# The softmax weights P of a top-k attention transposed by DMA through a DRAM scratch, in 26 of 32 head pairs, instead of by TensorE

## The chip, the cores and the metric

The kernel runs on one core of one Trainium2 chip. The metric is the device time of one execution in microseconds (us), the median over several runs. Five engines work side by side, each through its own instructions in order: TensorE (PE, with its weight loads shown apart as PEld), VectorE (DVE), ScalarE (ACT), GpSimd (POOL) and SyncE (SP), which here only issues DMAs. An engine waits only where its next instruction needs something that another engine or a DMA has not finished.

## The reference

Attention over 8 batches of 8 heads, 576 tokens, head size 64, in which each query keeps its 32 largest scores; then a Fourier mixing of the result and a two-layer MLP. All in 32-bit floats.

```python
scores = q @ k.T / sqrt(64)                      # per head: 576 x 576
kth = the 32nd largest score of each row
scores = where(scores >= kth, scores, -1e9)
attn = softmax(scores)                           # P, up to its denominator
x = (attn @ v) laid out as (batch, 576, 8 * 64)

mixed = real(fft(fft(x, axis=tokens), axis=channels))
u = x + mixed
un = (u - mean(u)) / sqrt(var(u) + 1e-6)
out = u + relu(un @ w_ch1) @ w_ch2               # 512 -> 2048 -> 512
```

## The kernel before

**Tiles.** The 64 heads are taken as 32 pairs, four pairs a batch. A pair is nine tiles of 128 query rows by 576 keys: blocks t = 0, 1, 2, 3 of 128 queries for head e = 0 and head e = 1, and one tile (t = 4, e None) that holds the last 64 queries of both heads. The order in a pair is t = 0, 0, 1, 1, 4, 2, 2, 3, 3. A batch has 36 tiles, the kernel 288.

**What happens to a tile.** PE computes the scores into PSUM (L369, and L339 for the last 64 keys), ACT copies them to SBUF as `S` (L372, L343, L361). DVE finds the 32 largest of each row: four MAX8 (L393) with three MATCH_REPLACE8 (L395) between them, writing to the work tile `wk`. `bounds` (L402, POOL) makes two numbers a row of the result. `mask` writes a large value to `wk` where the score is under the bound (Relu on ACT, L409) and subtracts that from the score (POOL, L412). `expo` (ACT, L418) takes the exponential in place in `wk`, with the row's sum. This is P, not yet normalised, with queries on the partitions.

The product with v needs P with keys on the partitions. `transposes` has PE transpose 128x128 blocks against an identity into PSUM (L439, four a tile; L450 and L454 for the last 64 keys) and ACT copy them to `PT` (L442, L451, L455, L457). `PT` has one buffer for each of two chunks of a pair: chunk 0 holds t = 0, 1, 4 (320 queries), chunk 1 holds t = 2, 3 (256 queries); each has nine blocks of 128 keys, four a head and one that both heads' last 64 keys share. `attend` (L476) multiplies PT by v in 20 matmuls into the PSUM tile `o`; ACT copies o to `xT` (L490); PE transposes it back (L516) and DVE normalises it into `x`.

**The Fourier part and the MLP** of a batch run while later batches are in attention: the foldings on POOL, the small transforms on PE (L667, L728), the MLP in units that the planner counts at about 1.8 to 2.7 us (`hidden`, L878, whose result ACT takes out of PSUM at L882; `back`, L905 and L944; and, once a batch, a product made of seven part products, L1075, for which halves and combinations of w2 are loaded again from DRAM by `bring`, L821).

**What sets the order.** The program is written out by hand for every engine, one step i a tile. In step i, PE computes the scores of tile i+3; ACT and POOL mask tile i-1 and take its exponential; PE transposes tile i-2; at the end of the step, if tile i-3 was the last of a chunk (position 4 or 8 in its pair), `attend` follows and ACT copies o to xT; DVE runs the last rounds of tile i and the first of tile i+1. Between these a planner places MLP units: `level` chooses a length for the step such that the queued units fit until the next batch's arrive, and `fixed_cost` is what it thinks PE needs for the attention work of a step (0.55 us of it for the transposes). In the first batch the transposes come a step earlier.

**Queues and buffers.** After the start, all loads and stores go through SP's queue, in program order: eight loads each of q, k and v for a pair (L236, L252, into the single buffer `nat`, or one of two of v), the MLP's w2 parts and the results. `S` has six buffers, `wk` three of a pair of tiles (one more for t = 4). PSUM has two banks for scores, two for transposes, one for `o`, three for the MLP.

Of the kernel before, what the change touches and what calls it, by code (L numbers as in the profile page):

```python
# [9 lines left out]
F32 = mybir.dt.float32  # L10
I32 = mybir.dt.int32
U32 = mybir.dt.uint32
AF = mybir.ActivationFunctionType
ALU = mybir.AluOpType

# [3 lines left out]
P = 128  # L19
TH = 32  # L20
# [52 lines left out]
def kernel(  # L73
# [9 lines left out]
    nc = tc.nc  # L83
    B, H, S, D = q.shape
# [5 lines left out]
    NF = NC - 1  # L90
    TAIL = 2 * TH
# [3 lines left out]
    NPB = H // 2  # L95
    NPAIR = B * NPB
# [5 lines left out]
    CW = (2 * P + TAIL, 2 * P)  # L102
    CHUNK_OF = {0: (0, 0), 1: (0, P), 4: (0, 2 * P), 2: (1, 0), 3: (1, P)}
# [10 lines left out]
    attp = ctx.enter_context(tc.tile_pool(name="attp", bufs=2))  # L114
    batp = ctx.enter_context(tc.tile_pool(name="batp", bufs=1))
    small = ctx.enter_context(tc.tile_pool(name="small", bufs=4))
    dramp = ctx.enter_context(
        tc.tile_pool(name="dram", bufs=1, space=bass.MemoryType.DRAM)
    )
# [53 lines left out]
    def weight_steps(chunks, space, wc, slots):  # L173

        def words(n):
            o = 2 * wc * (n % slots)
            raw = space[:, o:o + 2 * wc]
            return raw, raw[:, 0:2 * wc:2], raw[:, 1:2 * wc:2]
# [9 lines left out]
        def scale_high(n):  # L188
            if moe_w_ch1.dtype == F32:
                return  # L190
            nc.scalar.activation(
                out=chunks[n][0], in_=words(n)[2], func=AF.Copy, scale=2.0 ** -112
            )
# [9 lines left out]
        def rest(n):  # L203
            if moe_w_ch1.dtype == F32:
                return
            _, low, high = words(n)
            nc.scalar.activation(
                out=low.bitcast(I32), in_=low.bitcast(U32), func=AF.Copy, scale=2.0 ** -29
            )
            nc.scalar.activation(out=high, in_=high.bitcast(I32), func=AF.Sign)  # L210

# [13 lines left out]
    nat, qT_of, kT_of, v_of, PT, Ssb, Wk, Wp, M8, Nt = ({} for _ in range(10))  # L225
# [76 lines left out]
    PER_PAIR = len(IN_PAIR)  # L302
# [3 lines left out]
    items = [(pair, t, e) for pair in range(NPAIR) for t, e in IN_PAIR]  # L306
    N = len(items)
# [90 lines left out]
    def bounds(i):  # L398

        if i < N:  # L400
# [2 lines left out]
                out=Nt[i], in0=M8.pop(i)[:, 0:TOPK:TOPK - 1], in1=cc, op=ALU.mult  # L403
            )

    def mask(i, then=None):

        w = Wk[i]
        nc.scalar.activation(out=w, in_=Ssb[i], func=AF.Relu, scale=-FAR, bias=Nt[i][:, 1:2])  # L409
        if then is not None:  # L410
            then()
        nc.gpsimd.tensor_tensor(out=w, in0=Ssb.pop(i), in1=w, op=ALU.subtract)  # L412

    def expo(i):
        pair, t, e = items[i]
        w = Wk[i]
        c = DEN_COL[(t, e)]
        nc.scalar.activation(  # L418
            out=w, in_=w, func=AF.Exp, bias=Nt.pop(i)[:, 0:1],
            accum_out=den_t[pair % 3][:, c:c + 1],  # L420
        )

    def transposes(i):


        pair, t, e = items[i]
        p_sb = Wk.pop(i)
        ch, col = CHUNK_OF[t]
        if (pair, ch) not in PT:
            PT[pair, ch] = attp.tile(  # L430
                [P, 2 * NF + 1, CW[ch]], F32, name=f"PT_{pair}_{ch}", tag=f"PT{ch}", bufs=1
            )
        pt = PT[pair, ch]

        def full():
            k0 = TAIL if e == 1 else 0
            tp = ps_t.tile([P, 4, P], F32, name=f"tpP_{i}", tag="tp")
            for c in range(NF):
                nc.tensor.transpose(tp[:, c, :], p_sb[:, k0 + P * c:k0 + P * (c + 1)], ident)  # L439
            dsts = [(e, 0, P)] if e is not None else [(0, 0, TAIL), (1, TAIL, TAIL)]  # L440
            for he, o, w in dsts:
                nc.scalar.copy(  # L442
                    out=pt[:, NF * he:NF * (he + 1), col:col + w], in_=tp[:, :, o:o + w]
                )

        def tails():
            tp = ps_t.tile([P, 4, P], F32, name=f"tpP_{i}_t", tag="tp")
            if e == 1:
                both = Wp.pop(i - 1).rearrange("p e s -> p (e s)")[:, NF * P:S + TAIL]
                nc.tensor.transpose(tp[:, 0, :], both, ident)  # L450
                nc.scalar.copy(out=pt[:, 2 * NF, col:col + P], in_=tp[:, 0, :])  # L451
                return
            Wp.pop(i)
            nc.tensor.transpose(tp[:, 0, :], p_sb[:, S - P:S], ident)  # L454
            nc.scalar.copy(out=pt[TAIL:P, 2 * NF, col:col + TAIL], in_=tp[TAIL:P, 0, TAIL:P])  # L455
            for r in (0, TH):
                nc.scalar.copy(  # L457
                    out=pt[r:r + TH, 2 * NF, col:col + TAIL],
                    in_=tp[TAIL + r:TAIL + r + TH, 0, 0:TAIL],
                )  # L460

        full()
        if e != 0:
            tails()
        return 0.48 if e == 0 else 0.6

    def attend(pair, ch, c0=0, c1=None):

        c1 = CW[ch] if c1 is None else c1
        pt, vv = PT[pair, ch], v_of[pair]  # L470
        if c0 == 0:
            o_of[pair, ch] = ps_o.tile([P, CW[0]], F32, name=f"o_{pair}_{ch}", tag="o")
        o = o_of[pair, ch]
        for c in range(NC):
            for e in range(2):
                nc.tensor.matmul(  # L476
                    o[D * e:D * (e + 1), c0:c1],
                    lhsT=vv[:, c, e, :],
                    rhs=pt[:, 2 * NF if c == NF else NF * e + c, c0:c1],
                    start=(c == 0),  # L480
                    stop=(c == NC - 1),
                )
        return (c1 - c0) / 115.0

    def attended(pair, ch, late):
# [15 lines left out]

        nc.scalar.activation(out=rd[:, 0:n], in_=den[:, c0:c0 + n], func=AF.Copy, bias=1e-9)
        late.append(lambda: nc.vector.reciprocal(out=rd[:, 0:n], in_=rd[:, 0:n]))
# [780 lines left out]
    for o, place in ((B12, w2_12), (B21, w2_21)):  # L1284
        at(PER_BATCH + 14, "load2", lambda o=o, place=place: nc.sync.dma_start(
            out=scr[:, o], in_=place
# [3 lines left out]
    for b in range(B):  # L1290
# [47 lines left out]
        for n, t in enumerate((0, 1, 4, 2, 3)):  # L1338
            quick = first or last
            s = fc + (0 if first else n // 3 if last else n // 2)  # L1340
# [13 lines left out]

    def fixed_cost(i):

        t = 0.55 if 0 <= i - 2 < N else 0.0
        if i + 3 < N:
            t += {0: 1.04, 1: 0.3, None: 0.9}[items[i + 3][2]]
        if 0 <= i - 3 < N:  # L1360
            ch = {4: 0, 8: 1}.get((i - 3) % PER_PAIR)
            t += 0.0 if ch is None else (CW[ch] / 115.0 + 0.14 * len(CHUNKS[ch]))
        if i < N and i % PER_PAIR in (0, 5):
            t += 0.7
        return t + costs.get(i, 0.0)

    def level(i):

        steps = range(i, next((a for a in arrivals if a > i), i + PER_BATCH))
        rest, lev = sum(u[0] for u in queue + waiting), 0.0  # L1370
        while lev < 6.4 and sum(max(0.0, lev - fixed_cost(s)) for s in steps) < rest:
            lev += 0.02
        return lev

    def run(i, where):
        for fn in plan.pop((i, where), []):
            fn()
# [15 lines left out]
    i, carry = 0, 0.0  # L1393
    while i < N + 4 or plan or queue or sums:
# [3 lines left out]

        short = 0 <= i - 1 < PER_BATCH
        done = i - 1 if short else i - 2 if PER_BATCH <= i - 2 < N else None  # L1400

        fixed, j = [], i + 3
        e = items[j][2] if j < N else None
# [13 lines left out]
        if pending and pending[0][0] <= i and (  # L1419
            i < 2 * PER_BATCH + 4 or (i - 3) % PER_PAIR not in (4, 8)  # L1420
        ):
            _, pp, pc = pending[0]
# [12 lines left out]
        if short:  # L1435
            fixed += tok
            pair, r = divmod(i - 1, PER_PAIR)
            piece = {1: (0, 0, P), 4: (0, P, CW[0]), 6: (1, 0, P), 8: (1, P, CW[1])}.get(r)
            if piece is not None:
                fixed.append(lambda: attend(pair, *piece))  # L1440
            if i == PER_BATCH:
                fixed.append(lambda: attended(NPB - 1, 1, late_next) or 0.0)
                fixed.append(lambda: to_tokens(NPB - 1, 1, False))
        if i in arrivals:
            carry = min(carry, 0.0) if i > arrivals[0] else -5.0
            run(i, "units")
            step_us = level(i)
        room = step_us - carry - fixed_cost(i)
        cost, got = carry, 0.0
        run(i, "convert")  # L1450
        if short:
            expo(i - 1)
        for n, fn in enumerate(fixed):
            cost += fn()
            if n == n_mask:
                if PER_BATCH <= i - 1 < N:
                    mask(i - 1)
                run(i, "act")
                for fn in out_next:
                    fn()  # L1460
                out_next.clear()
            if n == min(n_tr, len(fixed) - 1) and PER_BATCH <= i - 1 < N:
                expo(i - 1)

            got += some(max(room * (n + 1) / len(fixed) - got, 1.1 if fn in preps else 0.0))
        if short:
            if piece is not None and r in (4, 8) and i < PER_BATCH:

                out_next.append(lambda pc=(pair, r // 8): attended(*pc, late_next))
                pending.append((i + 1, pair, r // 8))  # L1470

        soon_tile = 2 * PER_BATCH - 1
        for tile in (i - 3, i - 2):
            if not PER_BATCH <= tile < N or (tile == i - 2) != (tile == soon_tile):
                continue
            pair, r = divmod(tile, PER_PAIR)
# [27 lines left out]
        if i < PER_BATCH:  # L1504
            mask(i, lambda: run(i, "join"))
# [45 lines left out]
```

## Time and profile before

| | us |
|---|---|
| median of three runs | 1904.74 (1903.89 to 1906.25) |
| the profiled execution | 1907.16 |
| its span on the core | 1905.4 |
| period of a middle batch (36 tiles) | 214.4 |
| MAX8 and MATCH_REPLACE8 of one tile (three MAX8 of 0.749, one of 0.743, three MATCH_REPLACE8 of 0.742) | 5.2 |
| one exponential, with its accumulator read | 0.780 + 0.194 |
| one subtraction on POOL (L412) | 1.416 |
| one copy of four transposed blocks from PSUM to PT (L442, 512 columns) | 0.587 |

The mean granted TensorE clock of the profiled execution is 0.969 of full speed.

A page of the profile gives the busy time of each engine and its share of the span; the span in 40 slices, where a digit is the busy share in tenths; groups of instructions of one line with their count, their busy time in us, the mean duration of one in ns, and the idle time of the engine just before them with what ended it; and the DMA issues by line with KB each and the median us from issue to landing. Busy time of a group counts overlapping instructions once, so it is less than count times mean where instructions are pipelined, as on PE. A second kind of view gives the busy time of each engine in a stretch of the span, with the granted clock and the share of time that the 16 DMA engines were busy. A timeline gives start and duration of single instructions.

### The profile page before, as it was taken

Reading aid. Unit: us, or ns where it says so; the run is one execution under the profiler, and the core shown is the slowest. Engines: PE = TensorE matmul, PEld = TensorE weight load, DVE = VectorE, ACT = ScalarE, POOL = GpSimd, SP = SyncE. Lnnn points to the kernel's source line nnn. Section 1 sums busy time; section 2 is a strip of 40 time slices with the busy share of each in tenths; the row PEclk is TensorE's granted clock in tenths of the full one; section 3 lists DMA queues with packets and bytes.
Section 4 is the critical chain, followed back from the end, with each engine's and each line's share of the span. In section 5 each row is a group of like instructions: output and inputs, shape, how many; then the busy total and the mean of one; then the engine's idle time right before and its main releaser. Section 6 shows DMA issues by size and latency. Waiting matters only on the chain.

```text
span 1905.4 us, 28704 instructions
## 1 busy us (share of the span) xinstructions
PE 1790.4 (94%) x9200; PEld 1182.4 (62%) x9200; DVE 1585.3 (83%) x3301; ACT 1208.5 (63%) x3078; POOL 908.4 (48%) x1278
## 2 busy tenths in 40 slices
PE   5567799999899999999999999999999999999999
PEld 3344465474567756667567656667567656667678
DVE  7999999999899999989899888989899888872110
ACT  6878657776766767657676667666676667652100
POOL 4768643556535374345534464245534464241022
PEclk7787899999999999999999999999999999999999
DMA  5333001311104111131113101141113102030132
GB/s 165 104 94 108 20 13 50 99 56 25 41 14 130 34 25 47 42 107 28 25 47 98 53 20 52 35 114 27 25 47 97 53 19 57 25 103 6 50 101 80
DMA packets 184342, 111.25 MB, mean 58 GB/s; under 512 B 125952, under 2 KB 174208, under 8 KB 184192
## 3 DMA queue, kind: packets, MB, share of 16 engines
q1 hardware_dynamic: 183408, 109.20, 20.3%
q8 instruction: 74, 1.21, 0.3%
q14 instruction: 76, 0.62, 0.1%
q10 hardware_dynamic: 784, 0.21, 0.0%
HBM read 93.63 MB, written 15.73 MB: 57 GB/s over the span
## 4 chain that ended last, share of the span: by engine, by line
PE 80%; ACT 8%; DVE 6%; POOL 3%; issue 1%; DMA 1%; SPq 1%; POOLq 0%; DVEq 0%; ACTq 0%
PE hp L878 26%; PE cp L905 10%; PE o L476 8%; PE tpP L439 6%; PE sp L369 5%; PE cw L1075 5%; PE cv L1075 4%; PE yp L667 3%; PE cp L944 3%; DVE m L393 2%; DVE wk L395 2%; PE sp_t L339 2%; PE mp L728 2%; POOL wk L412 1%; ACT wk L409 1%
## 5 line engine op out<-in xcount | busy, mean ns | idle before, releaser
L412 POOL TENSOR_TENSOR wk<-S,wk 128x576 f32<-128x576 f32 x288 | 407.7, 1416 | 731.8 <-ACT wk L409 701.2
L393 DVE MAX8 m<-wk 128x8 f32<-128x576 f32 x864 | 626.3, 749 | 6.1
L878 PE MATMUL hp<-unT,w 128*128 128x256 f32 (+1 forms) x2048 | 539.9, 410 | 2.6 <-ACT unT L796 2.6
L878 PEld LDWEIGHTS hp<-unT,w 128*128 128x128 f32 x2048 | 374.3, 191 | 124.7 <-issue 25.8
L395 DVE MATCH_REPLACE8 wk<-m,wk 128x576 f32<-128x576 f32 x576 | 427.6, 742 | 0.0
L418 ACT ACTIVATE wk<-wk,nt 128x576 f32<-128x576 f32 x288 | 224.7, 780 | 75.6 <-POOL wk L412 74.5
L409 ACT ACTIVATE wk<-S,nt 128x576 f32<-128x576 f32 x288 | 226.8, 787 | 36.2 <-POOL nt L402 35.2
L439 PE MATMUL tpP<-ident,wk 128*128 128x128 f32 x1152 | 183.9, 284 | 67.3 <-ACT wk L418 40.7
L905 PE MATMUL cp<-w,hT 128*128 128x512 f32 x512 | 240.6, 598 | 0.0
L442 ACT COPY PT<-tpP 128x512 f32<-128x512 f32 (+1 forms) x320 | 171.2, 547 | 106.8 <-PE tpP L439 104.3
L393 DVE MAX8 m<-S 128x8 f32<-128x576 f32 x288 | 214.0, 743 | 21.6 <-ACT S L343 21.6
L439 PEld LDWEIGHTS tpP<-ident,wk 128*128 128x128 f32 x1152 | 141.2, 145 | 141.2 <-ACT wk L418 64.2
L882 ACT ACTIVATE hT<-hp 128x320 f32<-128x320 f32 (+1 forms) x256 | 104.7, 409 | 194.5 <-PE hp L878 192.1
L395 DVE MATCH_REPLACE8 wk<-m,S 128x576 f32<-128x576 f32 x288 | 213.7, 742 | 0.0
L476 PE MATMUL o<-PT,v 128*64 128x256 f32 (+3 forms) x1440 | 195.2, 414 | 1.9 <-ACT PT L442 1.8
L372 ACT COPY S<-sp 128x512 f32<-128x512 f32 (+1 forms) x264 | 141.7, 588 | 48.9 <-PE sp L369 48.6
L369 PE MATMUL sp<-kT,qT 64*128 64x512 f32 (+1 forms) x528 | 160.2, 666 | 4.8 <-ACT means L1263 3.3
L476 PEld LDWEIGHTS o<-PT,v 128*64 128x64 f32 x1440 | 111.4, 152 | 73.8 <-issue 16.7
L905 PEld LDWEIGHTS cp<-w,hT 128*128 128x128 f32 x512 | 88.8, 190 | 86.3 <-issue 86.2
L1020 POOL TENSOR_TENSOR hT<-hT 128x512 f32<-128x512 f32 x64 | 81.4, 1275 | 100.3 <-ACT hT L882 88.6
L1075 PE MATMUL cw<-w,hT 128*128 128x256 f32 x448 | 106.7, 383 | 1.4 <-POOL nt L402 1.2
L1075 PEld LDWEIGHTS cw<-w,hT 128*128 128x128 f32 x448 | 81.4, 190 | 18.9 <-issue 5.2
(157 smaller groups left out, 2179.3 us busy)
## 6 DMA issues: line engine op xcount, KB each, us to landing
w<-w_parts SPq DMA_DIRECT2D x82, 512.0 KB, 4.4
space<-in_moe_w_ch_dram SPq DMA_DIRECT2D x32, 512.0 KB, 3.5
nat<-in_q_dram SPq DMA_DIRECT2D x128, 64.0 KB, 2.1
v<-in_v_dram SPq DMA_DIRECT2D x128, 64.0 KB, 2.2
out_dram<-x SPq DMA_DIRECT2D x32, 256.0 KB, 2.1
nat<-in_k_dram SPq DMA_DIRECT2D x124, 64.0 KB, 2.2
w_parts<-w_t SPq DMA_DIRECT2D x8, 512.0 KB, 2.9
w_s<-w_parts SPq DMA_DIRECT2D x8, 512.0 KB, 4.8
```

What stands on the lines that cost most here:

```text
L369: nc.tensor.matmul(sp[r], lhsT=qT[hd, q_cols], rhs=kT[hd, :], start=True, stop=True)
L393: ops.append(lambda src=src, m8=m8: nc.vector.max(out=m8, in_=src))
L395: ops.append(lambda src=src, m8=m8: nc.vector.match_replace(w, m8, src, NEG))
L409: nc.scalar.activation(out=w, in_=Ssb[i], func=AF.Relu, scale=-FAR, bias=Nt[i][:, 1:2])
L412: nc.gpsimd.tensor_tensor(out=w, in0=Ssb.pop(i), in1=w, op=ALU.subtract)
L418: nc.scalar.activation(out=w, in_=w, func=AF.Exp, bias=Nt.pop(i)[:, 0:1], accum_out=den_t[pair % 3][:, c:c + 1],)
L439: nc.tensor.transpose(tp[:, c, :], p_sb[:, k0 + P * c:k0 + P * (c + 1)], ident)
L442: nc.scalar.copy(out=pt[:, NF * he:NF * (he + 1), col:col + w], in_=tp[:, :, o:o + w])
L476: nc.tensor.matmul(o[D * e:D * (e + 1), c0:c1], lhsT=vv[:, c, e, :], rhs=pt[:, 2 * NF if c == NF else NF * e + c, c0:c1], start=(c == 0), ...
L878: nc.tensor.matmul(hp[:, 0:w], lhsT=w1[:, dt, P * it:P * (it + 1)], rhs=unT[:, dt, 0:w], start=(dt == 0), stop=(dt == NDT - 1),)
L905: nc.tensor.matmul(cp, lhsT=hT[:, it, P * n:P * (n + 1)], rhs=w2[:, it, :], start=(it == 0), stop=(it == NIT - 1),)
L1075: nc.tensor.matmul(dst, lhsT=h()[a][:, kc, :], rhs=rhs_of(kc), start=start and kc == 0, stop=kc == NK - 1, skip_group_check=True,)
```

## The change

In pairs 4 to 30 except pair 7 (26 of 32), P is transposed by DMA. `expo` writes P not to `wk` but over the scores in `S`. `plane` copies it back to `wk` as two planes: first all low, then all high 16-bit halves of the row's 576 words, two strided copies on ACT, the first at the end of the step of the exponential (for tile i-1), the second at the start of the next (for tile i-2). It then writes the planes to a DRAM scratch in which a row is one query: 2 planes of 1152 values, the 576 of head 0 and the 576 of head 1 side by side (for t = 4 three writes bring the two heads together). After the second head, `turn` issues one DMA transpose of the (query, plane) rows, 256 rows of 1152 16-bit values (128 for t = 4), straight to PT, where low and high halves come to lie beside each other and form the 32-bit words again. All of these go through SP's queue. In those pairs `transposes` is not called: neither its PE transposes nor its ACT copies are there. The order of the instructions around them changes with it: the exponential now follows the last of a step's fixed PE pieces, which is often the only one. The shared block of PT moves from last to the middle, for all pairs. `fixed_cost` leaves out the 0.55 us in the pairs that changed. `attend` stays at its place.

```diff
--- before.py
+++ after.py
@@ -10,6 +10,7 @@
 F32 = mybir.dt.float32
 I32 = mybir.dt.int32
 U32 = mybir.dt.uint32
+U16 = mybir.dt.uint16
 AF = mybir.ActivationFunctionType
 ALU = mybir.AluOpType

@@ -403,21 +404,74 @@
                 out=Nt[i], in0=M8.pop(i)[:, 0:TOPK:TOPK - 1], in1=cc, op=ALU.mult
             )

+    def by_dma(i):
+
+        pair = i // PER_PAIR
+        return NPB <= pair < NPAIR - 1 and pair != 2 * NPB - 1
+
     def mask(i, then=None):

         w = Wk[i]
         nc.scalar.activation(out=w, in_=Ssb[i], func=AF.Relu, scale=-FAR, bias=Nt[i][:, 1:2])
         if then is not None:
             then()
-        nc.gpsimd.tensor_tensor(out=w, in0=Ssb.pop(i), in1=w, op=ALU.subtract)
+        nc.gpsimd.tensor_tensor(out=w, in0=Ssb[i], in1=w, op=ALU.subtract)
+        if not by_dma(i):
+            Ssb.pop(i)

     def expo(i):
         pair, t, e = items[i]
         w = Wk[i]
         c = DEN_COL[(t, e)]
         nc.scalar.activation(
-            out=w, in_=w, func=AF.Exp, bias=Nt.pop(i)[:, 0:1],
+            out=Ssb[i] if by_dma(i) else w, in_=w, func=AF.Exp, bias=Nt.pop(i)[:, 0:1],
             accum_out=den_t[pair % 3][:, c:c + 1],
+        )
+
+    planes_of = {}
+
+    def plane(i, half):
+
+        if not (0 <= i < N and by_dma(i)):
+            return
+        words = Wk[i].bitcast(U16).rearrange("p (h s) -> p h s", h=2)
+        src = Ssb[i].bitcast(U16).rearrange("p (s h) -> p h s", h=2)
+        nc.scalar.copy(out=words[:, half, :], in_=src[:, half, :])
+        if half == 0:
+            return
+        Ssb.pop(i)
+        Wk.pop(i)
+        pair, t, e = items[i]
+        nq = TAIL if e is None else P
+        if e != 1:
+            planes_of[pair, t] = dramp.tile(
+                [nq, 2, 2 * S], U16, name=f"planes_{pair}_{t}", tag="planes", bufs=3
+            )
+        to = planes_of[pair, t]
+        if e is not None:
+            nc.sync.dma_start(out=to[:, :, S * e:S * (e + 1)], in_=words)
+        else:
+            nc.sync.dma_start(out=to[:, :, 0:S], in_=words[0:nq])
+            nc.sync.dma_start(out=to[:, :, S:S + TAIL], in_=words[nq:P, :, NF * P:S])
+            nc.sync.dma_start(out=to[:, :, S + TAIL:2 * S], in_=words[nq:P, :, 0:NF * P])
+        if e != 1:
+            Wp.pop(i)
+
+    def turn(i):
+
+        if not (0 <= i < N and by_dma(i)) or items[i][2] == 0:
+            return
+        pair, t, e = items[i]
+        src = planes_of.pop((pair, t))
+        ch, col = CHUNK_OF[t]
+        if (pair, ch) not in PT:
+            PT[pair, ch] = attp.tile(
+                [P, 2 * NF + 1, CW[ch]], F32, name=f"PT_{pair}_{ch}", tag=f"PT{ch}", bufs=1
+            )
+        pt, nq = PT[pair, ch], src.shape[0]
+        nc.sync.dma_start_transpose(
+            out=pt[:, :, col:col + nq].bitcast(U16),
+            in_=src.rearrange("q h s -> (q h) s"),
         )

     def transposes(i):
@@ -440,7 +494,7 @@
             dsts = [(e, 0, P)] if e is not None else [(0, 0, TAIL), (1, TAIL, TAIL)]
             for he, o, w in dsts:
                 nc.scalar.copy(
-                    out=pt[:, NF * he:NF * (he + 1), col:col + w], in_=tp[:, :, o:o + w]
+                    out=pt[:, (NF + 1) * he:(NF + 1) * he + NF, col:col + w], in_=tp[:, :, o:o + w]
                 )

         def tails():
@@ -448,14 +502,14 @@
             if e == 1:
                 both = Wp.pop(i - 1).rearrange("p e s -> p (e s)")[:, NF * P:S + TAIL]
                 nc.tensor.transpose(tp[:, 0, :], both, ident)
-                nc.scalar.copy(out=pt[:, 2 * NF, col:col + P], in_=tp[:, 0, :])
+                nc.scalar.copy(out=pt[:, NF, col:col + P], in_=tp[:, 0, :])
                 return
             Wp.pop(i)
             nc.tensor.transpose(tp[:, 0, :], p_sb[:, S - P:S], ident)
-            nc.scalar.copy(out=pt[TAIL:P, 2 * NF, col:col + TAIL], in_=tp[TAIL:P, 0, TAIL:P])
+            nc.scalar.copy(out=pt[TAIL:P, NF, col:col + TAIL], in_=tp[TAIL:P, 0, TAIL:P])
             for r in (0, TH):
                 nc.scalar.copy(
-                    out=pt[r:r + TH, 2 * NF, col:col + TAIL],
+                    out=pt[r:r + TH, NF, col:col + TAIL],
                     in_=tp[TAIL + r:TAIL + r + TH, 0, 0:TAIL],
                 )

@@ -476,7 +530,7 @@
                 nc.tensor.matmul(
                     o[D * e:D * (e + 1), c0:c1],
                     lhsT=vv[:, c, e, :],
-                    rhs=pt[:, 2 * NF if c == NF else NF * e + c, c0:c1],
+                    rhs=pt[:, NF if c == NF else (NF + 1) * e + c, c0:c1],
                     start=(c == 0),
                     stop=(c == NC - 1),
                 )
@@ -1354,7 +1408,7 @@

     def fixed_cost(i):

-        t = 0.55 if 0 <= i - 2 < N else 0.0
+        t = 0.55 if 0 <= i - 2 < N and not by_dma(i - 2) else 0.0
         if i + 3 < N:
             t += {0: 1.04, 1: 0.3, None: 0.9}[items[i + 3][2]]
         if 0 <= i - 3 < N:
@@ -1398,6 +1452,8 @@

         short = 0 <= i - 1 < PER_BATCH
         done = i - 1 if short else i - 2 if PER_BATCH <= i - 2 < N else None
+        if done is not None and by_dma(done):
+            done = None

@@ -1447,6 +1503,8 @@
             step_us = level(i)
         room = step_us - carry - fixed_cost(i)
         cost, got = carry, 0.0
+        plane(i - 2, 1)
+        turn(i - 2)
         run(i, "convert")
         if short:
             expo(i - 1)
@@ -1469,6 +1527,7 @@
                 out_next.append(lambda pc=(pair, r // 8): attended(*pc, late_next))
                 pending.append((i + 1, pair, r // 8))

+        plane(i - 1, 0)
         soon_tile = 2 * PER_BATCH - 1
         for tile in (i - 3, i - 2):
             if not PER_BATCH <= tile < N or (tile == i - 2) != (tile == soon_tile):
```

## The prediction

> **What bounds the kernel now.** I read the page's busy shares and its slices first, then the busy time of single batches, then the waits of one middle batch.
>
> ```profile
> PE 1790.4 (94%) x9200; PEld 1182.4 (62%) x9200; DVE 1585.3 (83%) x3301; ACT 1208.5 (63%) x3078; POOL 908.4 (48%) x1278
> ...
> PE   5567799999899999999999999999999999999999
> ...
> DVE  7999999999899999989899888989899888872110
> ```
>
> DVE is full for 36 of 40 slices and stops where attention stops (near 1714 us); the last 190 us are TensorE alone and the change does not touch them. The shares of the whole span therefore hide what matters. By stretches (length, then PE, PEld, DVE, ACT, POOL busy, clock, DMA share, GB/s; second batch, third batch, one middle batch, last batch):
>
> ```profile
> 240.00:470.00 230.00, 219.68 (x1071) 132.89 (x1070) 216.29 (x447) 155.67 (x421) 112.02 (x162) 0.99 0.17 49
> 470.00:686.00 216.00, 207.09 (x1119) 139.68 (x1121) 201.94 (x419) 148.33 (x386) 107.70 (x164) 0.98 0.20 52
> 936.05:1150.47 214.42, 213.15 (x1131) 141.29 (x1132) 192.71 (x401) 145.40 (x372) 104.61 (x156) 1.00 0.19 51
> 1542.00:1714.00 172.00, 170.50 (x889) 111.04 (x888) 143.81 (x300) 108.37 (x276) 77.66 (x107) 1.00 0.19 53
> ```
>
> A middle batch takes 214.4 us for 36 tiles (5.96 us a tile). PE is busy 99% of it and sets the time; DVE follows at 90%, ACT at 68%. So work taken off PE shortens the batch, but only until the next engine is full: never below DVE's 192.7.
>
> **The change, part by part** (per middle batch of 4 pairs; 26 pairs change in all).
>
> *Removed from PE.* Groups of the same middle batch and of the page:
>
> ```profile
> L439 PE MATMUL tpP<-ident,wk 128*128 128x128 f32 x144 | 21.7, 273 | 0.0
> L450 PE MATMUL tpP_t<-ident,wk 128*128 128x128 f32 x16 | 4.4, 273 | 0.0
> L454 PE MATMUL tpP_t<-ident,wk 128*128 128x128 f32 x4 | 1.1, 273 | 0.0
> ```
>
> 21.7 + 4.4 + 1.1 = 27.2 us of PE's path; PE falls to 213.2 - 27.2 = 186 us and stops being the longest.
>
> *Removed from and added to ACT.* The instructions that write PT are 68 ACT copies, 26.5 us of busy time in that batch. Added are two copies of 128x576 16-bit values for each of 36 tiles. The trace has no such copy; the nearest is a copy from SBUF to SBUF that reads every second word and converts integers:
>
> ```profile
> L207 ACT ACTIVATE space<-space 128x512 int32<-128x512 uint32 x32 | 21.4, 669 | 0.0
> ...
> L418 ACT ACTIVATE wk<-wk,nt 128x576 f32<-128x576 f32 x288 | 224.7, 780 | 75.6 <-POOL wk L412 74.5
> ```
>
> 669 ns at 512 columns, plus 64 columns at 0.83 ns (L442 takes 587 ns at 512 columns and 386 at 256, 0.8 ns a column), is 0.72 us. Bounds: 0.59 us (a 512-wide copy out of PSUM) and 0.97 (the exponential with its accumulator read, 780 + 194 ns). I take 0.72, less 0.03 because neighbours overlap (two copies of 588 ns end in 1.06 us): 72 x 0.69 = 49.7. ACT's busy time goes 145.4 - 26.5 + 49.7 = 168.6 us.
>
> *A wait that comes with it.* The exponential of a tile needs POOL's subtraction, which needs ACT's own Relu:
>
> ```profile
> 999.57 0.80 ACT L409 ACTIVATE wk<-S,nt 128x576 f32<-128x576 f32 x1
> ...
> 1000.45 1.41 POOL L412 TENSOR_TENSOR wk<-S,wk 128x576 f32<-128x576 f32 x1 [3.25 <-ACT wk L409]
> ...
> 1001.90 0.78 ACT L418 ACTIVATE wk<-wk,nt 128x576 f32<-128x576 f32 x1 [1.05 <-POOL wk L412]
> ```
>
> From Relu's end (1000.37) to the exponential's start is 1.53 us, in which ACT idles unless other copies stand between. PT copies often stood there; now the exponential is issued straight after the Relu in 14 of a batch's 36 tiles. Taking 1.53 less the ACT work between the two, tile by tile in the instruction order, gives 34 us a batch after and 12 before; the trace shows 7.2 of those 12. I take 28 (bounds 20, the measured ratio, and 34). Behind the waiting exponential stand the Relus of the hidden layer and the score copies, so PE waits for PSUM banks next. ACT's own floor is 168.6 + 28 + 4.8 (the wait for o before xT that it has today) = 201 us: above DVE's 192.7 and PE's 186. ACT becomes the longest.
>
> *Added DMAs.* Per batch 32 writes of 288 KB and 12 smaller ones to DRAM, and 20 transposes, 16 of 576 KB and 4 of half that, all on SP's queue. How long a plain DMA takes is in the issues; how much a packet costs is in two stretches, 1013.5 to 1018.5 us (only 256-byte rows in flight) and 1023 to 1044 us (1 KB rows):
>
> ```profile
> out_dram<-x SPq DMA_DIRECT2D x32, 256.0 KB, 2.1
> nat<-in_k_dram SPq DMA_DIRECT2D x124, 8.0 KB, 1.7
> ```
> ```profile
> q1 hardware_dynamic: 1278, 0.30, 26.5%
> ```
> ```profile
> q1 hardware_dynamic: 2783, 2.77, 46.6%
> ```
>
> 16 engines x 5 us x 0.265 / 1278 = 16.6 ns for a 256-byte packet; 16 x 21 x 0.466 / 2783 = 56 ns for 1 KB. No row shows a DMA transpose. If it reads its 576 KB as 2304 packets of 256 bytes, that is 2304 x 16.6 / 16 = 2.4 us, plus the 1.7 us that an 8 KB load needs to land: 4.1 us. Bounds: 3.3 (576 KB at the best slice, 359 GB/s, plus 1.7) and 9.8 (each packet at the 56 ns of a 1 KB one, 8.1 + 1.7). I take 4.1, the row of the same packet size, and keep both ends. Bandwidth is no limit at that price: 36 tiles x 256 packets x 63 ns / 16 = 36 us and 18 x 2.4 = 43 us beside today's 0.19 x 214 = 41, 120 us of some 207.
>
> One rule speaks against the change: the Trainium skill, "VectorE: DVE Perf Modes", section "The three transpose paths", puts a 128x128 two-byte block at 390 ns on TensorE and 1309 ns by DMA, and recommends TensorE where PSUM will do. TensorE's row here is 21.7 / 144 = 0.15 us for a whole 32-bit block; a transpose of the change holds 18 two-byte blocks, so by the page, with nothing overlapping, it would take 23.6 us and the kernel would end near 2,840 us. I do not take it: 1.3 us for one small DMA is less than the 1.7 us of the smallest loads here, so most of it must be fixed cost, paid once a DMA.
>
> *Whether the transposes arrive in time.* A tile's second plane copy opens step i, the attend that needs it closes step i+1: two steps, 11.5 us at 207 us a batch. In them lie the copy 0.7, the write's landing 2.1, the transpose 4.1 and the attend's 20 matmuls 2.9 (ACT waits for them at xT): 9.8. SP must also issue eight q, k or v loads ahead of some of these, 0.48 us each:
>
> ```profile
> 1013.75 1.92 SPq L236 DMA_DIRECT2D nat<-in_k_dram  x4
> ```
>
> That is 3.8 us, of which I let 1.0 fall into the chain: 10.8, leaving 0.7 us. The write also frees the tile's half of wk, where a transpose on PE did; with three pairs of wk in rotation its next user comes six steps later, which covers it. S is freed a step later, and its next writer is ACT itself, later in ACT's own order: nothing. The loads themselves, needed four or more steps later, are covered by that distance; the reloads of w2 halves that queue behind a transpose have two or more product parts between load and use. If the cover is gone, every microsecond late is paid by ACT and PE at both chunks of a pair: 52 us of span per us, at most.
>
> **The sum.** Three engines now stand at 186, 193 and 201 us; today's idle DVE time (21.7 us) shows how loosely they run, and I add a quarter of it, 5.5: 207 us a middle batch, 7.4 less. The planner's 0.55 us less a step spreads the same MLP units and moves no work between batches. Four such batches give 30. The third batch has 9 us more DVE work (201.9): 210, 6 less. The second (three pairs changed, DVE already 94%) 4 less. The last (three pairs) 7.4 x 27/36, 5 less. Together 45: the profiled span of 1905.4 becomes 1860. That execution took 1907.2, the runs' median is 1904.7; 45 less is **1860 us**. Its own range: 198 us a middle batch (DVE, with a quarter of its idle time) gives -92 in all, 1813; 212 gives about -14, 1890.
>
> **Rivals.**
> *Late transposes.* The wait for DMA takes the place of the transposes on PE. For it: no row prices a transpose, the slack is 0.7 us, and SP's queue holds loads, writes and transposes in one order, each transpose waiting for its write. Against it: 256-byte packets are cheap here. It decides from 0.9 us late on (45 / 52), a transpose of 5.7 us. At 7 us it is 2.2 late, 114 us: 1975. At the bound of 9.8 it is 5 late, 260 us: 2120.
> *ACT is fuller still.* At 0.97 us a plane copy ACT's floor is 219, the batch 222, some 50 us more than before over six and a half batches: 1955. For it: 72 copies replace 68, of twice the length; against: ACT's conversion copy above shows 669 ns.
> *Nothing is left of it.* Relief on PE is eaten by ACT's waits and by small delays of attends: 214 us a batch, 1905. For it: the floor of 201 is only 6% away; against: PE's 27 us is really gone.
>
> **How the numbers follow.** The forecast has 0.46, all faster. Late transposes 0.32, slower. ACT fuller 0.12, of which 0.10 slower and 0.02 faster. Nothing left 0.10: 0.05 within 0.2%, about what a measurement tells from no change, 0.03 slower, 0.02 faster. So faster 0.50, same 0.05, slower 0.45. The likeliest case is 1860 (1813 to 1890); for 8 in 10 the range must reach into the late transposes, to 2050 (a transpose of some 8.4 us), leaving about 1 in 10 above and 1 in 20 below 1815.
>
> **What would show it.** Right: a transpose lands about 4 us after issue, PE near 186 and ACT busy near 169 us a middle batch, a period of 203 to 212. Wrong: long waits of PE's attend matmuls, or of ACT at xT, on the transposes' DMA; transposes landing after 6 us or more; plane copies well off 0.7 us; the exponential waiting for POOL far from 28 us a batch.

## The result, and the profile after

The changed kernel is slower: median 2122.21 us (2118.12 to 2126.56, four runs) against 1905.49 (1903.89 to 1908.09, four runs), ratio 1.1136 with a 95% interval of 1.111 to 1.1162. The profiled execution took 2126.6 us, its span is 2124.7.

The page of the changed kernel, busy time and slices:

```profile
PE 1761.9 (83%) x8134; PEld 1112.9 (52%) x8134; DVE 1591.1 (75%) x3301; ACT 1316.3 (62%) x3104; POOL 906.4 (43%) x1278
...
PE   5666977788887878878888789888889789899999
...
DVE  8999977687876878786778688787888787773300
PEclk7778988898898999998999899999999899999999
```

No engine is full in the second to eighth batch: PE and DVE mostly stand at 7 or 8 tenths where they stood at 8 or 9. Every engine waits for something else. ACT is busy no longer than forecast, so it is not full either. One middle batch before, and one after, from the last MAX8 of a batch to that of the next (columns as in the prediction's view of stretches). It is the longest of the four: they take 230, 256, 246 and 238 us, where they took 208, 213, 214 and 214:

```profile
842.60:1056.00 213.40, 212.13 (x1127) 141.12 (x1125) 191.55 (x399) 144.29 (x371) 104.42 (x155) 1.00 0.19 50
```
```profile
946.50:1202.20 255.70, 208.91 (x964) 129.47 (x964) 193.18 (x400) 162.01 (x378) 105.49 (x157) 0.92 0.51 129
```

DVE and POOL did the same work in the same busy time, so nothing became slower in itself there. The batch is 42 us longer, PE is busy 209 us and not the 186 of the forecast, and the granted TensorE clock fell from 1.00 to 0.92. What the engines waited for, over the whole changed kernel (us in total, times, longest):

```profile
ACT S L426 <- POOL wk L418: 232.2, 194, 10.1
...
ACT xT L544 <- PE o L530: 214.4, 35, 15.1
...
PE o L530 <- DMA PT<-planes: 97.4, 26, 13.2
...
PE cp L998 <- DMA w<-w_parts: 35.9, 4, 11.8
```

The same rows before: ACT waited 39.3 us at xT and 74.5 us for POOL ahead of the exponential (POOL wk L412), and PE 1.1 us for reloads of w2. New, then, are a late product with v (second and third row), late w2 reloads (fourth), and the wait for POOL that the forecast had counted. The transposes themselves are quick. DMA issues and ACT's plane copies of the changed kernel:

```profile
planes<-wk SPq DMA_DIRECT2D x208, 288.0 KB, 2.6
...
PT<-planes SPq DMA_TRANSPOSE x130, 4.6
```
```profile
L439 ACT COPY wk<-S 128x576 uint16<-128x576 uint16 x468 | 294.6, 668 | 3.9
```

A transpose lands 4.6 us after its issue (median). Why it is late all the same is in the timeline of SP's queue, around the writes of one t = 4 tile:

```profile
816.67 2.86 SPq L472 DMA_TRANSPOSE PT<-planes  x1
819.62 2.06 SPq L237 DMA_DIRECT2D nat<-in_q_dram  x4
821.78 1.80 SPq L253 DMA_DIRECT2D nat<-in_q_dram  x4
823.69 0.58 SPq L454 DMA_DIRECT2D planes<-wk  x1
824.31 0.60 SPq L455 DMA_DIRECT2D planes<-wk  x1
824.96 0.61 SPq L456 DMA_DIRECT2D planes<-wk  x1
827.51 1.30 SPq L472 DMA_TRANSPOSE PT<-planes  x1
828.86 2.11 SPq L237 DMA_DIRECT2D v<-in_v_dram  x4
```

The transpose of the tile before holds the queue for 2.86 us, eight q loads for 3.9, and only then do this tile's three writes go out, half a microsecond and more each; the transpose waits 1.9 us more for the last of them to land. Its product with v and then xT come after that, while ACT stands still:

```profile
831.26 4.61 PE L530 MATMUL o<-PT,v 128*64 128x320 f32 x20 [4.56 <-DMA PT<-planes]
...
835.91 0.43 ACT L544 COPY xT<-o 128x320 f32<-128x320 f32 x1 [5.13 <-PE o L530]
```

The product itself takes longer too. In the middle batch before, one took 2.91 us (L476, at 999.61 us) at a granted clock of 1.00; this one takes 4.61, at 0.64. The matmuls of chunk 0's products in pairs 4 to 31, before and after:

```profile
L476 PE MATMUL o<-PT,v 128*64 128x320 f32 x560 | 83.5, 442 | 0.0
```
```profile
L530 PE MATMUL o<-PT,v 128*64 128x320 f32 x560 | 133.7, 636 | 135.2 <-DMA PT<-planes 69.9 <-issue 27.6 <-DVE wk L396 21.8
```

That is 50 us more of PE for the same 28 products, while the hidden layer's matmuls hardly changed (410 ns before, 416 after).

From the records of all 26 changed pairs, means in us:

| | chunk 0 | chunk 1 |
|---|---|---|
| from the second plane copy's end to its write (t = 4: the third write) | 5.7 | 0.8 |
| from that write's start to the transpose's issue | 2.6 | 2.7 |
| SP held by that transpose | 1.3 (half size) | 2.5 |
| from the transpose's issue to the first matmul of the product | 4.2 | 5.0 |
| length of the product | 4.9 (before 3.0) | 2.7 (before 2.4) |
| ACT idle before xT | 7.2 (before 0.9) | 0.5 (before 0.4) |

Chunk 0 is late, by SP's queue; chunk 1 is almost in time. 26 x (7.2 + 0.5) = 200 us of ACT idle at xT, against 32 before.

Not all of it is the transposes'. In the last pair of each middle batch (pairs 15, 19, 23 and 27) ACT idles 11 to 15 us before chunk 0's xT, and in three of these four PE has first stood 10.5 to 11.8 us for a reload of w2, which goes out only behind loads, writes and a transpose:

```profile
944.18 2.02 SPq L237 DMA_DIRECT2D nat<-in_q_dram  x4
...
951.98 1.31 SPq L472 DMA_TRANSPOSE PT<-planes  x1
953.39 1.07 SPq L875 DMA_DIRECT2D w<-w_parts  x2
...
958.21 2.82 PE L998 MATMUL cp<-w,hT 128*64 128x512 f32 x5 [11.83 <-DMA w<-w_parts]
```

### The profile page after: what moved, and what is told of

Same layout as the page of the kernel before. It is cut to its first block, busy times and chain, and to the rows that moved or that the text cites. A ratio compares the mean times of both kernels' runs of the same rounds, so it can differ in the third digit from the quotient of the medians.

```text
span 2124.7 us, 27548 instructions
## 1 busy us (share of the span) xinstructions
PE 1761.9 (83%) x8134; PEld 1112.9 (52%) x8134; DVE 1591.1 (75%) x3301; ACT 1316.3 (62%) x3104; POOL 906.4 (43%) x1278
## 4 chain that ended last, share of the span: by engine, by line
PE 38%; DVE 14%; issue 13%; ACT 12%; POOL 10%; DMA 10%; SPq 3%; POOLq 0%; DVEq 0%; ACTq 0%
PE hp L932 11%; PE o L530 7%; DVE m L394 7%; DVE wk L396 6%; POOL wk L418 5%; PE cp L959 4%; DMA planes<-wk 4%; DMA PT<-planes 3%; PE yp L721 3%; ACT wk L439 2%; PE cw L1129 2%; ACT S L426 2%; PE cp L998 2%; ACT wk L415 2%; PE sp L370 2%
## 5 line engine op out<-in xcount | busy, mean ns | idle before, releaser
L932 PEld LDWEIGHTS hp<-unT,w 128*128 128x128 f32 x2048 | 383.5, 194 | 145.9 <-issue 38.5
L530 PE MATMUL o<-PT,v 128*64 128x256 f32 (+3 forms) x1440 | 252.2, 500 | 177.8 <-DMA PT<-planes 97.4
L426 ACT ACTIVATE S<-wk,nt 128x576 f32<-128x576 f32 x234 | 181.5, 776 | 232.6 <-POOL wk L418 232.2
L439 ACT COPY wk<-S 128x576 uint16<-128x576 uint16 x468 | 294.6, 668 | 3.9
L530 PEld LDWEIGHTS o<-PT,v 128*64 128x64 f32 x1440 | 143.1, 180 | 282.8 <-issue 165.0
L557 DVE RECIPROCAL rd<-rd 128x6 f32<-128x6 f32 x64 | 11.6, 182 | 228.9 <-ACT rd L556 228.9
L370 PE MATMUL sp<-kT,qT 64*128 64x512 f32 (+1 forms) x528 | 164.9, 671 | 13.2 <-ACT kT L294 4.9
L544 ACT COPY xT<-o 128x320 f32<-128x320 f32 x64 | 25.5, 399 | 214.6 <-PE o L530 214.4
L998 PE MATMUL cp<-w,hT 128*64 128x512 f32 x256 | 71.9, 650 | 35.9 <-DMA w<-w_parts 35.9
```

Source lines behind the costliest of these rows:

```text
L370: nc.tensor.matmul(sp[r], lhsT=qT[hd, q_cols], rhs=kT[hd, :], start=True, stop=True)
L426: nc.scalar.activation(out=Ssb[i] if by_dma(i) else w, in_=w, func=AF.Exp, bias=Nt.pop(i)[:, 0:1], accum_out=den_t[pair % 3][:, c:c + 1],)
L439: nc.scalar.copy(out=words[:, half, :], in_=src[:, half, :])
L530: nc.tensor.matmul(o[D * e:D * (e + 1), c0:c1], lhsT=vv[:, c, e, :], rhs=pt[:, NF if c == NF else (NF + 1) * e + c, c0:c1], start=(c == 0) ...
L932: nc.tensor.matmul(hp[:, 0:w], lhsT=w1[:, dt, P * it:P * (it + 1)], rhs=unT[:, dt, 0:w], start=(dt == 0), stop=(dt == NDT - 1),)
```

## The experiments

Theory A was that SP's queue makes the transposes of chunk 0 late and that this is the loss. The rivals: B, ACT's waits for POOL; C, the transpose itself; later D, the traffic as such. Each run is one execution, except the last; the kernel before took 1904.9 to 1908.9 us on the same chips.

**Loads out of the way.**

```diff
-            if i % PER_PAIR == 5:
+            if i % PER_PAIR == 6:
                 load_nat("q", pair_of + 2)
-            if i % PER_PAIR == 6:
+            if i % PER_PAIR == 7:
                 load_v(pair_of + 1)
```

> The q loads of a pair move from the end of step 5 to the end of step 6, the v loads from step 6 to step 7, so that they no longer stand in SP's queue between the transpose of position 3 and the writes of position 4. Theory A (SP's queue is late: chunk 0's last write starts 5.7 us after its plane copy, and ACT waits 7.2 us at xT for chunk 0 in each of 26 pairs): the delay falls to some 1 us, ACT's wait at chunk 0 to about 2.5, 26 x 4.7 = 120 us less: about 2000 us. Rival B (the time goes to ACT's waits for POOL between Relu and exponential, 232 us in all, and DMA is not the bound): within 20 us of 2122. Rival C (a DMA transpose is slow in itself): within 20 us of 2122, and the wait at xT stays.

Measured: 2053.98 us, 68 less. The delay of chunk 0's last write fell from 5.7 to 2.4 us and ACT's idle before xT from 7.2 to 3.5, while that of chunk 1 rose from 0.5 to 0.9. Only the order of loads was touched, so neither B nor C can be the whole loss. The size was overrated: the write is still 2.4 us late and not 1, and of the 91 us of idle time left for chunk 0, 44 are in the four pairs named above.

```profile
ACT xT L544 <- PE o L530: 126.1, 44, 11.9
```

**More cover for chunk 0.**

```diff
-        for tile in (i - 3, i - 2):
+        for tile in (i - 4, i - 3, i - 2):
...
+            if (tile == i - 4) != (r == 4 and by_dma(tile)):
+                continue
```

> Chunk 0's product with v comes one step later in the changed pairs (three steps of cover instead of two); SP's queue stays as it is. Theory A: about 6 us more cover against 7.2 us of wait at xT for chunk 0, so nearly all of 26 x 7.2 = 188 us goes: 1930 to 1970 us. Rival B: within 20 us of 2122. Rival C: gains as well, but chunk 1, which keeps its two steps, waits as long as chunk 0 did; by theory A chunk 1 stays at its 0.7 us.

Measured: 2096.70 us, 26 less where 150 to 190 were expected: a miss for A. ACT's idle before xT did go for chunk 0 (7.2 to 1.6 us), but it came back elsewhere. Waits of this run:

```profile
ACT S L373 <- PE sp L370: 67.3, 19, 15.3
...
PE cp L998 <- DMA w<-w_parts: 50.0, 5, 13.3
```

PE stood for w2 reloads (50 us, 36 before this edit), and ACT behind it for scores. This points to a second loss in the same queue, which the late product had partly covered; the runs without reloads below test it.

**No DMA at all.** Pair 4's PT is kept and multiplied with v in pairs 5 to 30. Pair 7 has no transposes on TensorE either, here and in the other runs of this kind below.

```diff
...
+        if pair > NPB:
+            PT[pair, ch] = kept[ch]
+            return
         src = planes_of.pop((pair, t))
...
```

> Leaves out the writes and DMA transposes of all pairs but pair 4, whose PT is multiplied with v in pairs 5 to 30 (pair 7 included, whose TensorE transposes are left out too); the plane copies on ACT stay. It shows what ACT, POOL, DVE and PE leave without any DMA. Theory A: 1850 to 1900 us, the ACT wait at xT for o back near the 39 us of before. Rival B: 2050 us or more, since ACT's plane copies and its waits for POOL are all still there. Rival C agrees with A here.

Measured: 1892.90 us. All of the loss goes with the DMAs, although ACT keeps its plane copies and its waits for POOL, so B falls. What is left is 16 us below before, not the 45 of the forecast. Stretch and waits of this run:

```profile
858.00:1072.00 214.00, 203.11 (x981) 127.41 (x983) 192.14 (x399) 160.77 (x378) 105.58 (x157) 0.98 0.21 56
```
```profile
ACT S L426 <- POOL wk L418: 239.6, 202, 2.6
...
ACT xT L552 <- PE o L538: 26.0, 12, 6.5
```

From one batch's last MAX8 to the next the seven batches take 227, 211, 206, 214, 206, 204 and 218 us (before: 214, 206, 208, 213, 214, 214, 222). Of the middle ones three reach the forecast's 207 and one does not; together these four gain 21 us where 30 were forecast. The second and third lose 13 and 5 us. PE is busy 192 to 203 us in the middle batches, 93 to 97% of them, and ACT 157 to 161: PE is still the fullest engine, with DVE (191 to 192) close behind. The tail after the last MAX8 takes 190 us where it took 198.

**The exponential later.**

```diff
-            if n == min(n_tr, len(fixed) - 1) and PER_BATCH <= i - 1 < N:
+            if n == min(n_tr, len(fixed) - 1) and PER_BATCH <= i - 1 < N and not by_dma(i - 1):
                 expo(i - 1)
...
+        if PER_BATCH <= i - 1 < N and by_dma(i - 1):
+            expo(i - 1)
         plane(i - 1, 0)
```

> The exponential of a tile in the changed pairs is issued at the end of the step, after the step's score copies and hidden-layer Relus, instead of after the last fixed PE piece, so that ACT has work while POOL subtracts. Theory A: the wait for POOL falls from 232 to below 100 us, but ACT then waits longer at xT, since the planes come later: within 40 us of 2122, either way. Rival B: 100 us or more faster, about 2000 us.

Measured: 2125.64 us, the same. The wait for POOL fell from 232 to 146 us and ACT waited 64 us longer for the hidden layer's results (178 us instead of 114). Against B again.

**Both earlier edits together.**

> Both earlier edits together: q and v loads one step later, and chunk 0's product with v one step later. If the late chunk is what is left (91 us of ACT's wait at xT for chunk 0 remained with the loads moved, 42 with the product moved), both are removed: 2054 - 60 to 90, about 1965 to 2000 us. If what is left are the reloads of w2 halves behind the transposes (one wait of 9 to 13 us of PE a batch in both earlier runs) and contention of DMAs, 2030 us or more.

Measured: 2090.86 us, 37 slower than the loads alone. The first reading missed; the second's "2030 us or more" holds, but neither had this run slower than the loads alone. Moving chunk 0's product moves work between PE's steps without the planner knowing; that this is the reason was not tested, and why the later product costs time stays open.

**All DMAs, but no reader.** Each transpose goes back to the work tile that it came from.

```diff
...
+        if pair > NPB:
+            pt = work.rearrange("p e s -> p (e s)").rearrange("p (c q) -> p c q", c=2 * NF + 1)
+            col = 0
         nc.sync.dma_start_transpose(
```

> As the run without DMA, but all writes and DMA transposes are issued again, each transpose back into the work tile that it came from, where nothing reads it; products with v in pairs 5 to 30 still take pair 4's PT. It keeps SP's queue and the memory traffic of the change and takes away only that PE waits for a transpose. Theory A (lateness of PT on the path is the main loss): 1893 plus one w2 reload wait of 9 to 13 us in each of some seven batches, 1950 to 1985 us. Rival D (the traffic itself slows the engines or the other loads): 2050 us or more. If the reloads are harmless too: 1893 to 1915.

Measured: 2006.00 us: 116 less than the change and 113 more than without DMA, above A's 1950 to 1985. Busy times are those of the run without DMA (DVE 1589.5 against 1585.3 us, ACT 1313.1 against 1313.2) although the DMA engines are busy 57% of a middle batch, so traffic as such slows neither of the two. PE waits, of this run:

```profile
PE cp L1004 <- DMA w<-w_parts: 44.7, 5, 10.9
...
PE cw L1135 <- DMA w<-w_parts: 19.7, 6, 5.5
```

DVE also waited 29.8 us for transposes that came back to the work tiles, which is this edit's own cost.

**The same without w2 reloads.**

```diff
     def bring(o, place, part):
+        if not isinstance(place, list) and now[0] < N:
+            return
...
```

> As the run with unread transposes (same parts left out), and the reloads of w2 halves during attention are left out too (the products then use what stands in w2). If the w2 reloads that queue on SP behind writes and transposes are what the traffic costs there (PE waited 64 us for them): 2006 - 60, about 1945 us. If the traffic costs time by itself: within 20 us of 2006.

Measured: 1914.43 us, 92 less where some 60 were expected, and within 22 of the run without DMA, with every write and transpose still in flight. D falls. What the queue costs beside the transposes' own lateness is w2 reloads behind them: in the run that has them they land about as fast as before (4.9 us after issue, 4.4 before), so it is their issue that is late. The edit also takes 72 of the 82 transfers of 512 KB out of the traffic. Against the run without DMA only the second batch is clearly longer (254 us against 227).

**The change without w2 reloads.** The same edit on the change.

> The change as it is, but the reloads of w2 halves during attention are left out (the products use what stands in w2). If the reloads' lateness and the transposes' lateness add up, as 92 us for the first (2006 to 1914 without a reader of the transposes) suggest: about 2030 us. If most of the time the one hides in the other, since both make PE and ACT wait in the same steps: 2070 to 2110.

Measured: 2069.56 us: 53 less, not 92. The two latenesses partly hide in each other: ACT's idle time before chunk 0's xT falls from 7.2 to 5.7 us, nearly all of it in the four pairs named above (to 4 to 6 us there). With the reloads, taking the reader away is worth 116 us; without them 155 (2069.56 to 1914.43).

**No DMA, and the exponential later.**

> As the run without DMA (the same parts left out), with the exponential at the end of the step. If ACT's waits for POOL (240 us in the run without DMA) set the time there, as the forecast's floor for ACT says, they fall to some 130 us and the time by 50 to 100 us: 1795 to 1845. If DVE and PE hold the time at that level, within 15 us of 1893.

Measured: 1887.43 us, 5 less. The wait for POOL fell to 146 us and the wait for the hidden layer rose from 88 to 157. The edit exchanged one wait of ACT for another, so the wait for POOL does not by itself set the time, and PE is busy 93 to 97% of the middle batches here too.

**The last 64 queries on TensorE.** The tile of t = 4 keeps its transposes; chunk 1's product one step later except in a batch's last pair; k loads one step later.

```diff
-        return NPB <= pair < NPAIR - 1 and pair != 2 * NPB - 1
+        return NPB <= pair < NPAIR - 1 and pair != 2 * NPB - 1 and items[i][2] is not None
...
```

> The tile of the last 64 queries goes back to TensorE transposes in the changed pairs, so the last DMA transpose of chunk 0 has three steps of cover; chunk 1's product comes one step later except in the last pair of a batch, and the k loads one step later. Theory A: no waits for PT are left (ACT's wait at xT near the 39 us of before), only the w2 reloads: 1950 to 1985 us. Rival D: 2030 us or more.

Measured: 1963.36 us, 159 less than the change, as A expected, though ACT still waited 58.9 us at xT and not about 39. Chunk 0's products are back at 437 ns a matmul. The middle batches take 214 to 216 us where they took 208 to 214; the second and third take 247 and 228. Three things were changed at once, so the run does not say what each of them won.

**Stores of w2 combinations from ACT's queue**, in addition.

```diff
-        at(now[0] + 1, "load2", lambda: nc.sync.dma_start(out=scr[:, 0:4, kc, :], in_=t))
+        at(now[0] + 1, "load2", lambda: nc.scalar.dma_start(out=scr[:, 0:4, kc, :], in_=t))
```

> As the run with the last 64 queries on TensorE, with the eight stores of w2 combinations in the second and third batch issued from ACT's queue instead of SP's. If the second and third batch (33 and 22 us longer there than before the change) are slow because POOL waits 42 us for these stores behind SP's transposes: POOL's wait falls to some 14 us and the time to about 1935. If not: within 10 us of 1963.

Measured: 1948.44 us, 15 less; the second batch fell from 247 to 234 us, POOL's wait for these stores only from 42.5 to 34.3. So that is a part of the second batch's loss, and half of what was expected of it.

**Blocks t = 0 and 1 alone**, four of nine tiles, transposed at the end of the step. Pair 7 is changed too, and the stores of w2 combinations stay on ACT's queue.

```diff
+        return NPB <= pair < NPAIR - 1 and items[i][1] in (0, 1)
...
-        turn(i - 2)
         run(i, "convert")
...
+        turn(i - 2)
         if i < N:
```

> Only blocks t = 0 and 1 (four of nine tiles) go by DMA, in pairs 4 to 30; the transpose is issued at the end of its step, when the write has landed, with three steps and more before chunk 0's product; the w2 combinations are stored from ACT's queue. TensorE keeps 5/9 of its transposes (213 - 12 = 201 us a middle batch), ACT gains about 10 + 12 us. If TensorE's relief is real and only its balance with ACT and SP's queue was missed: below both kernels, 1850 to 1895 us. If SP's queue still delays loads and stores: 1910 to 1950.

Measured: 1910.98 us, at the lower end of what was expected if SP's queue still delays. Waits for transposes are no longer among PE's longest, and the sixth and seventh batch take 210 and 211 us where they took 214, but the second takes 225 where it took 214.

**The same from the third batch on.**

> As the run with blocks t = 0 and 1 alone, from pair 8 on (the third batch), with all stores on SP's queue again. In that run the third to seventh batch took 1269 us to the last MAX8 against 1279 before, the second batch 11 us more than before. If the second batch goes back to its 214 us: 1895 to 1902 us, below both kernels. If the relief of PE only moves to the tail (201 us there against 198): 1903 to 1912.

Measured in twelve runs against seventeen of before: 1907.27 us against 1907.44, ratio 1.0005 (0.9994 to 1.0015). No difference, as expected if the relief only moves to the tail. (The 1269 and 1279 us of the expectation are those of the third to the eighth batch.) The second batch is back at 213 us, middle batches take 205 to 217, and the tail after the last MAX8 is 201 us instead of 198. No version was found that beats the kernel before by more than a measurement can tell; even the runs that leave the transposes' DMAs out stand only 1% below it.

## Why the prediction was wrong

The step that failed is *Whether the transposes arrive in time*. Three of its terms were about right. Plane copy 0.7 us: measured 0.67. Write 2.1: measured 2.6. Transpose 4.1: measured 4.6 at full size, and 3.5 for the half-size one that chunk 0 waits for. The term that failed is "SP must also issue eight q, k or v loads", of which 1.0 us was let into the chain. For chunk 0, whose last tile follows the transpose of the tile before and the q loads in the same queue, the write goes out 5.7 us after its data is ready. The issue of a transpose was priced at nothing on SP; it holds the queue for 2.5 us. And the product after the wait takes 4.9 us, not 2.9. So the slack was not +0.7 us but the chunk was 7.2 us late by ACT's idle before xT (5.7 us in the run without w2 reloads).

"52 us of span per us, at most" holds as a bound for both chunks together: chunk 0 alone would be 26 x 7.2 = 188, and the run without a reader puts the lateness of PT at 116 us with the w2 reloads present and 155 without.

"The reloads of w2 halves that queue behind a transpose have two or more product parts between load and use" was the second failure, in the same paragraph: that cover is gone when a reload stands behind loads, writes, their landing and a transpose. PE waits 10.5 to 11.8 us in each of three batches, and leaving the reloads out takes 53 us off the change and 92 where no product waits for PT.

ACT's part held in size: 168.6 us busy a middle batch was forecast, 162 measured; 28 us of waits for POOL, 35 measured in the batch shown. PE's did not: 186 us was forecast, and 192 to 203 measured without DMA. The 27.2 us taken off are busy times of groups that overlap their neighbours. In the trace before, four transposes at 999.07 us last 0.62 us, but the next matmul starts 0.54 us after they began; counted from each start to the next, the 164 transposes of that batch take 19 us. So without DMA PE is still fuller than ACT, and ACT's floor of 201 us was not by itself what bound the batch: putting the exponential later took 90 us of its waits for POOL away and only 5 us of time. That the middle batches came to 204 to 206 us there, but for one of 214, beside a forecast of 207, is therefore in part luck.

The sum's other batches were wrong even without DMA: 4 and 6 us less were forecast for the second and third batch, 13 and 5 more came. In the second, pair 4 still has its DMAs in that run, and ACT idles 6.5 us before its chunk 0's xT; POOL's waits for w2 stores are shorter than before there (8.8 us, 13.8 before). How the 13 us divide was not settled. That the planner "moves no work between batches" did not hold either: 341 of the hidden layer's matmuls are left for the tail after the last MAX8 where 368 were, and the tail takes 190 us instead of 198.

The rival *Late transposes* named the right place, and asked for a transpose of 5.7 us to decide. The transpose took 4.6 us and it was decided by the queue ahead of it. Its bound of 9.8 us is refuted, and that its 2120 us lies beside the measured 2122 is luck: it stood for slow transposes, late by 5 us at both chunks. Bandwidth was no limit, as forecast: 120 us of DMA time a batch was forecast, and 57% of 225.6, 129 us, measured in the run without a reader, most of whose loss goes with the reloads.

The Trainium skill's 1309 ns for a small block ("VectorE: DVE Perf Modes", section "The three transpose paths") was rightly not multiplied by 18: 4.6 us a transpose of 576 KB, not 23.6. Its advice to use TensorE, which stands in the section "Rules for kernel authors" of that page, held here for another reason than its price.

## What to carry to other kernels

Before work is moved from a full engine to DMAs, add up the issuing queue as one adds up an engine: each issue (here 0.4 to 0.6 us), each wait for a write to land (2.6 us) and each transpose's hold (2.5 us), in program order, and look for what urgent transfer stands behind them. A fuller queue delays not only the new transfers but every old one that shares it. Count a relief of a pipelined engine from start to next start, not by busy time: here 27 us a batch were 19, and without any DMA a middle batch became at most 8 to 10 us shorter. And a wait on PE can cost twice: the product after it took 4.9 us instead of 3.0.

## What the runs showed of the hardware

A DMA transpose of 256 rows of 1152 16-bit values from DRAM to SBUF lands 4.6 us after issue (median; 4.4 to 6.2), and one of half the rows after 3.5 (3.4 to 3.7). It holds SP's queue 2.5 us (1.3 at half the rows). It reads in packets of 256 bytes: the trace holds 380,160 packets of exactly that size against 110,592 before, 269,568 more, which is 104 x 2304 + 26 x 1152.

The granted TensorE clock is lower where PE waits more, though not by PE's busy share alone: in a middle batch 1.00 before (PE busy 99%), 0.98 without DMA (95%), 0.96 with unread transposes (90%), 0.97 with the loads later (85%), 0.92 in the change (82%); over the span 0.969 and 0.915. It falls in stretches: in the batch shown of the change it stood at 0.5 for six stretches of 6.8 to 13.7 us and at 1.00 between them. The product shown above, after 4.6 us of waiting, ran at 0.64 and took 4.61 us, where one before ran at 1.00 and took 2.91. Matmuls that follow such waits are slower on average (chunk 0's product 636 ns against 442, the part behind w2's reloads at L998 650 against 603), and those of the hidden layer are not (416 against 410). The product's 26 x (4.9 - 3.0) = 49 us are a part of the loss of 217 us that no run separates from the wait itself.
